# Routing attention and an ELU layer on one core: row sums of two blocks in one group of matmuls, masks of q on ScalarE, first k cut at 512 tokens

## The chip, the core and the metric

The kernel runs on one core of a Trainium2 chip. The core has a matrix engine (TensorE, PE in the profile), three engines for elementwise work (VectorE or DVE, ScalarE or ACT, GpSimd or POOL), a queue that issues transfers (SyncE or SP), and 16 DMA engines. Each engine works through its own instructions in program order and waits on semaphores for the others. TensorE writes into banks of PSUM; the other data lie in SBUF, with 128 partitions. The metric is device time in microseconds (us) of one execution, as a median over runs.

## The reference

```python
def _attn_ref(q, k, v, centroids):            # q, k, v: (4, 8, 768, 64)
    ...
    q_assign = np.argmax(np.einsum('bhsd,hcd->bhsc', q_n, c_n), axis=-1)
    k_assign = np.argmax(np.einsum('bhsd,hcd->bhsc', k_n, c_n), axis=-1)
    mask = q_assign[:, :, :, None] == k_assign[:, :, None, :]
    scores = scale * np.matmul(q, k.transpose(0, 1, 3, 2))
    scores = np.where(mask, scores, -1000000000.0)
    ...
    attn = np.exp(scores)
    attn = attn / (np.sum(attn, axis=-1, keepdims=True) + 1e-09)
    return np.matmul(attn, v).astype(np.float32)

def _moe_ref(x, w_in, w_out):                 # x: (3072, 512), w_in: (512, 2048)
    h = x @ w_in
    g = np.where(h > 0.0, h, np.exp(np.minimum(h, 0.0)) - 1.0)
    return (g @ w_out).astype(np.float32)
```

Each token of q and of k is given to the nearest of 16 centroids of its head, and a query sees only keys of its own cluster. The attention's output, with heads side by side, then goes through two matrix products with an ELU between them. The two weight matrices come as 64-bit floats; the kernel takes their words apart and joins them to 32-bit floats itself.

## The kernel before

**Blocks and slots.** The attention is cut into 32 blocks: batch (4), half of the queries (2), pair of heads (4). `slot_first` handles block 0 and `slot(n)` block n, for n = 1 to 31. In a slot TensorE computes, for each of six tiles of 128 keys, the scores of both heads (`plain`, L498) and adds the mask to them by a second product (`masked`, L511); ScalarE exponentiates 768 columns at once (`exponential`, L520). The keys lie on partitions and the 384 queries of the half along the free dimension. Three pairs of PSUM banks (`pair_tiles`) take the scores in turn.

**One block behind: the values.** At the start of slot n TensorE multiplies the probabilities of block n-1 with v (`values`, L536), into `o_bank`; ScalarE takes the result out, negated, into its place in `xT` (`take_values`, L550). `x_of(n)` is that place.

**Two blocks behind: row sums and division.** VectorE adds the six tiles of probabilities of a block into `summed` (`sums_begin`, L523; `sums_end`, L528 and L529). TensorE sums that over the partitions with a matrix of ones (`row_sums`, L554): one matmul for each head, 64 output partitions each, so that a row sum stands on all 64 partitions that need it, in `d_bank`. ScalarE reads them as a logarithm and as a copy, and forms the exponential of the negative logarithm (`take_sums`, L563 to L565). VectorE refines the reciprocal by one Newton step, with the sign that take_values left out (`divide`, L568, L569), and GpSimd multiplies x by it (L572). `d_bank` is used by the clusters too.

**Clusters.** `similar` (L427) multiplies the centroids with tokens: four matmuls of 32 output partitions each, into `d_bank` (or `o_bank` in the first slot). VectorE finds the greatest by transposes, a maximum and a comparison (`assign`, L440 to L453), with counts for a later check that each token has one cluster. ScalarE copies the result to the other half of the partitions (L456), and for q GpSimd makes 0 and -2^80 of it (`mask_q`, L463). q is treated in slots 1 and 5 of each batch (slot 3 instead of 1 in the first), k in slots 6 and 7 for the next batch. What is put into the list `later` (copies, masks, power steps) is issued by `flush` at the end of the slot.

**Weights.** `weigh(n)` puts some steps of the weights into each slot by a fixed table of room and cost (`ROOM`, `COST`): `begin` (L320, L328) separates words, ScalarE scales the exponents (L330, the power step, through `later`), and three `join` steps on VectorE (L340, L344, L350) put them together. What is left is done in the first group after the attention.

**Loads.** All plain loads are issued by SyncE in program order: v of the next block (`load_v`, L182), k and q of the next batch in small packets (`in_blocks`, L166), words of the weights (L300). The loads of the first k and q (L191) are laid out differently and are transposed on TensorE (`turned`, L577, copied out by ScalarE, L594).

**After the attention.** `finish_attention` is called within the first of four units (`unit(0, u)`) of the first group of 512 tokens, and handles the last block. In these units GpSimd works on weights (`w_step`, L727 to L732, with transfers to DRAM) and on the ELU (L762). Five groups more follow from 400 us on, in a scheme that the change leaves alone.

Of the kernel before, what the change touches and what calls it, by code (L numbers as in the profile page):

```python
# [61 lines left out]
def main_path(ctx, tc, c, q, k, v, centroids, moe_w_in, moe_w_out, out):  # L62
# [71 lines left out]
    top = early[:, 7488:7512]  # L134
    hot_q = early[:, 7512:7896].bitcast(BF16).rearrange("p (s n) -> p s n", s=2)
# [3 lines left out]
    summed = sums_w[:, 4 * HS : 6 * HS]  # L139
# [111 lines left out]
    cT = const.tile([P, P], F32, name="cT")  # L251
    count = const.tile([P, 4 * B], F32, name="count")
    counted = 0
    r_sum = const.tile([P, len(blocks)], F32, name="r_sum")
    d_sum = const.tile([P, len(blocks)], F32, name="d_sum")
    off = const.tile([P, 1], F32, name="off")
    nc.gpsimd.memset(off, -896.0 * 2**23)
# [52 lines left out]
    def begin():  # L310
# [19 lines left out]
        later.append(lambda: nc.scalar.activation(e, e, Act.Relu, scale=8.0, bias=off))  # L330
# [63 lines left out]
    credit, later = 0.0, []  # L394

    def flush():
        for other in later:
            other()
        later.clear()
# [25 lines left out]
    def similar(t, cols, ps):  # L425
        for pr in range(NPR):
            nc.tensor.matmul(  # L427
                ps[32 * pr : 32 * pr + 32, :HS],
                lhsT=cT[:, 32 * pr : 32 * pr + 32],
                rhs=t[pr][:, cols],  # L430
                start=True,
                stop=True,
            )

    def assign(hot, ps):
# [3 lines left out]
        n = HS // NC  # L439
        nc.vector.transpose(sim, ps[:, :HS])  # L440
# [20 lines left out]
    def mask_q(half):  # L461
        for x in range(2):
            nc.gpsimd.tensor_scalar(  # L463
                q_mask[half][:, :, x],
                hot_q,
                big[:, x : x + 1],
                minus[:, x : x + 1],
                op0=Alu.mult,
                op1=Alu.add,
            )  # L470

    def clusters_k(b, half, ps):
        cols = ts(half, HS)
# [3 lines left out]
    def clusters_q(b, half, ps):  # L477
        similar(qT[half], slice(0, HS), ps)

        def told():  # L480
            assign(hot_q, ps)
            later.append(lambda: mask_q(half))
# [4 lines left out]
    turn_of = 0  # L487
# [39 lines left out]
    def sums_end():  # L527
        nc.vector.tensor_tensor(add_to, add_to, probs_all[:, 8 * HS :], op=Alu.add)  # L528
        nc.vector.tensor_tensor(  # L529
            summed, add_to[:, : 2 * HS], add_to[:, 2 * HS :], op=Alu.add  # L530
# [21 lines left out]
    def row_sums(n):  # L552
        for e in range(2):
            nc.tensor.matmul(  # L554
                d_bank[64 * e : 64 * e + 64, :HS],
                lhsT=ones,
                rhs=summed[:, ts(e, HS)],
# [4 lines left out]
    def take_sums(n):  # L562
        nc.scalar.activation(r_of, d_bank[:, :HS], Act.Ln)  # L563
        nc.scalar.activation(e_of, d_bank[:, :HS], Act.Copy, accum_out=d_sum[:, n : n + 1])
        nc.scalar.activation(r_of, r_of, Act.Exp, scale=-1.0)  # L565

    def divide(n):
        nc.vector.tensor_tensor(e_of, e_of, r_of, op=Alu.mult)  # L568
        nc.vector.scalar_tensor_tensor(  # L569
            r_of, e_of, -2.0, r_of, op0=Alu.add, op1=Alu.mult, accum_out=r_sum[:, n : n + 1]  # L570
        )
        nc.gpsimd.tensor_tensor(x_of(n), x_of(n), r_of, op=Alu.mult)  # L572
# [8 lines left out]
    def turn(to, t, n):  # L581

        for i in range(HT):
            turned_by_pe(to[:, ts(i, P)], t, n + i)

    turns = 0

    def turned(to, t, n):
# [4 lines left out]
        turn(bank, t, n)  # L593
        nc.scalar.copy(to, bank[:, :HS])  # L594

    def slot_first():
# [10 lines left out]
        for pr in range(NPR):  # L607
            turned(kT[0][pr][:, :HS], first_k[pr], 0)
        told = [clusters_k(0, 0, o_bank)]
        flush()  # L610
        for pr in range(NPR):
            turned(kT[0][pr][:, HS:], first_k[pr], HT)
# [8 lines left out]
        for kt in range(NT):  # L621
            s = ring()
            plain(0, kt, s)
# [8 lines left out]
    def slot(n):  # L632
        b, at = n // NB, n % NB
        more = b + 1 < B
        if n > 1:
            row_sums(n - 2)
            take_sums(n - 2)
# [9 lines left out]
        if n > 0:  # L647
            sums_end()
        if n > 1:
            divide(n - 2)  # L650
        if n > 0:
            take_values(n - 1)
        if told is not None:
            told()

# [28 lines left out]
        flush()  # L684
# [678 lines left out]
    def findings():  # L1363
# [6 lines left out]
        nc.vector.tensor_scalar(ok[:, 1:2], peak[:, 1:2], D_MAX, None, op0=Alu.is_lt)  # L1370
        nc.vector.tensor_scalar(same, count, float(HS // NC), None, op0=Alu.is_equal)
# [10 lines left out]
    last_n = len(blocks) - 1  # L1382
# [14 lines left out]
    row_sums(last_n - 1)  # L1397
    values(last_n)
    sums_end()
# [316 lines left out]
```

## Time and profile before

| what | value |
|---|---|
| median of 3 runs | 901.79 us (900.97 to 903.19) |
| the profiled execution | 902.24 us, span 900.5 us |
| TensorE clock | 0.999 |
| attention, first group, rest | about 0 to 341, 341 to 400, 400 to 900 us |
| L554, row sums | 128 records (each f32 matmul leaves two), median 512 ns |
| L572, x by reciprocals (GpSimd) | 32, mean 1103 ns |
| L463, masks (GpSimd) | 16, from 983 to 3039 ns |
| L520, exponentials (ScalarE) | 192, mean 811 ns |
| L330, power step (ScalarE) | 16, median 1148 ns |
| L563, L564, L565 (ScalarE) | 32 each, median 479, 481 and 522 ns |
| L569 (VectorE) | 32, median 558 ns |

Busy time in stretches of the run (us), from the view that cuts the run into windows:

| from, to | TensorE | VectorE | ScalarE | GpSimd |
|---|---|---|---|---|
| 0, 20 | 17.36 | 9.30 | 10.80 | 3.06 |
| 20, 40 | 19.36 | 12.22 | 13.22 | 1.00 |
| 100, 200 | 100.00 | 96.84 | 76.42 | 20.59 |
| 200, 300 | 99.08 | 96.94 | 75.34 | 25.65 |
| 350, 375 | 25.00 | 23.05 | 11.54 | 18.47 |
| 700, 900 | 194.17 | 137.89 | 74.53 | 39.64 |

How to read it: an f32 matmul shows as two records; records that run side by side on different parts of the array overlap, so their durations do not add up, and the distance between starts is the better measure. In a timeline each row merges instructions of one line that follow each other: start, length, engine, line, operation, what it writes and reads, the tile of the array, shape, count, and in brackets the idle time before it with what ended it.

### The profile page before, as it was taken

The numbers are of one execution on the slowest core, as the hardware profiler recorded it, in microseconds if no ns is written. First come the engines' busy times: TensorE is split into PE (matmuls) and PEld (weight loads), VectorE is DVE, ScalarE is ACT, GpSimd is POOL, SyncE is SP. The second block draws the span as 40 slices with busy tenths as digits, with TensorE's granted clock in tenths as the row PEclk, the third lists the DMA queues.
The fourth block names the chain that finished last, engine by engine and source line by source line (L and its number), as shares of the span: only waits on it lengthen the run. The fifth ranks groups of instructions, "written<-read, shape, count | busy, mean of one in ns | idle before, by whom it ended". The sixth has DMA issues, their size and how long they took to land.

```text
span 900.5 us, 17050 instructions
## 1 busy us (share of the span) xinstructions
PE 889.9 (99%) x6473; PEld 687.6 (76%) x6473; DVE 725.9 (81%) x1067; ACT 449.5 (50%) x883; POOL 226.0 (25%) x257
## 2 busy tenths in 40 slices
PE   8999999999999999999999999999999999999997
PEld 4444444444444447899989999999999999999997
DVE  4699999999999997995389965895589558956885
ACT  5677787777776774420133225522552255225421
POOL 1022031221303244870033002520252025202300
PEclk9999999999999999999999999999999999999999
DMA  6765554365323622102698766176717761767272
GB/s 197 195 110 137 153 137 80 105 135 139 71 82 96 192 88 71 70 13 95 199 296 302 241 206 220 50 242 206 218 55 241 212 210 58 240 210 209 58 221 87
DMA packets 153209, 138.33 MB, mean 154 GB/s; under 512 B 89248, under 2 KB 106656, under 8 KB 152096
## 3 DMA queue, kind: packets, MB, share of 16 engines
q1 hardware_dynamic: 151584, 132.45, 50.2%
q0 software_dynamic: 1248, 4.20, 1.5%
q8 instruction: 53, 0.87, 0.4%
q10 hardware_dynamic: 288, 0.52, 0.2%
q14 instruction: 36, 0.29, 0.1%
HBM read 114.59 MB, written 21.50 MB: 151 GB/s over the span
## 4 chain that ended last, share of the span: by engine, by line
PE 92%; DVE 4%; DMA 2%; SPq 1%; issue 0%; ACT 0%; DVEq 0%
PE bank L994 23%; PE bank L748 16%; PE banks L498 12%; PE o_bank L536 12%; PE bank L1066 9%; PE o_bank L994 4%; PE o_bank L748 3%; PE banks L511 3%; PE d_bank L994 2%; PE d_bank L554 2%; PE o_bank L1066 2%; PE d_bank L427 1%; SPq L166 1%; DMA w_out<-in_k_dram 1%; PE d_bank L1066 1%; PE d_bank L748 1%
## 5 line engine op out<-in xcount | busy, mean ns | idle before, releaser
L520 ACT ACTIVATE p_out<-banks 128x768 f32<-128x768 f32 x192 | 155.2, 811 | 26.8 <-PE banks L511 25.4
L536 PE MATMUL o_bank<-p_out,kq_g 128*64 128x384 f32 x768 | 129.4, 486 | 0.1
L536 PEld LDWEIGHTS o_bank<-p_out,kq_g 128*64 128x64 f32 x768 | 55.0, 137 | 69.2 <-issue 62.7
L762 POOL TENSOR_SCALAR kq_g<-kq_g 128x512 f32<-128x512 f32 x96 | 67.8, 715 | 152.0 <-ACT kq_g L761 151.6
L572 POOL TENSOR_TENSOR xT<-xT,sums_w 128x384 f32<-128x384 f32 x32 | 35.3, 1103 | 222.0 <-DVE sums_w L569 164.6
L523 DVE TENSOR_TENSOR sums_w<-p_out 128x1536 f32<-128x1536 f32 x32 | 57.1, 1785 | 7.5 <-ACT p_out L520 7.5
L994 PE MATMUL bank<-w_out,kq_g 128*128 128x128 f32 x512 | 63.1, 275 | 0.0
L528 DVE TENSOR_TENSOR sums_w<-sums_w,p_out 128x1536 f32<-128x1536 f32 x32 | 59.0, 1845 | 3.3 <-DVE sums_w L523 0.5
L994 PEld LDWEIGHTS bank<-w_out,kq_g 128*128 128x128 f32 x512 | 60.5, 192 | 0.5
L761 ACT ACTIVATE kq_g<-bank 128x512 f32<-128x512 f32 x68 | 39.8, 602 | 38.9 <-PE bank L748 17.3
L748 PE MATMUL bank<-xT,spare 128*128 128x256 f32 x256 | 59.2, 379 | 0.0
L748 PEld LDWEIGHTS bank<-xT,spare 128*128 128x128 f32 x256 | 48.3, 190 | 6.4
L748 PE MATMUL bank<-x_sum,w_in 128*128 128x256 f32 x224 | 52.9, 379 | 0.0
L765 DVE SCALAR_TENSOR_TENSOR kq_g<-kq_g,bank 128x512 f32<-128x512 f32 x68 | 44.9, 680 | 6.2 <-POOL kq_g L762 6.2
L748 PEld LDWEIGHTS bank<-x_sum,w_in 128*128 128x128 f32 x224 | 42.6, 190 | 5.8
L1280 DVE TENSOR_TENSOR kq_g<-kq_g 128x1024 f32<-128x1024 f32 x36 | 45.2, 1263 | 1.5 <-PE bank L994 1.5
L1084 POOL TENSOR_TENSOR spare<-x_sum 128x128 f32<-128x128 f32 x16 | 7.3, 455 | 154.4 <-PE bank L1066 88.8
L463 POOL TENSOR_SCALAR kq_g<-w_out,big,minus 128x768 bf16<-128x768 bf16 x16 | 34.1, 2138 | 46.8 <-ACT w_out L456 46.8
L550 ACT ACTIVATE xT<-o_bank 128x384 f32<-128x384 f32 x32 | 15.7, 490 | 48.3 <-PE o_bank L536 48.3
L498 PE MATMUL banks<-x_sum,xT 64*128 64x384 f32 x192 | 39.8, 492 | 0.0
L498 PE MATMUL banks<-x_sum,kq_g 64*128 64x384 f32 x192 | 39.6, 491 | 0.0
L498 PE MATMUL banks<-kq_g 64*128 64x384 f32 x192 | 39.6, 491 | 0.0
(326 smaller groups left out, 2030.2 us busy)
## 6 DMA issues: line engine op xcount, KB each, us to landing
kq_g<-in_v_dram SPq DMA_DIRECT2D x32, 384.0 KB, 3.6
sums_w<-far_s_s SPq DMA_DIRECT2D x42, 256.0 KB, 3.7
spare<-w_far SPq DMA_DIRECT2D x32, 256.0 KB, 3.1
words_w<-far_s_s SPq DMA_DIRECT2D x26, 256.0 KB, 3.5
out_dram<-p_out SPq DMA_DIRECT2D x22, 256.0 KB, 3.4
w_out<-in_q_dram SPq DMA_DIRECT2D x112, 48.0 KB, 2.7
sums_w<-far_s_q SPq DMA_DIRECT2D x21, 256.0 KB, 3.6
words_w<-far_a_s SPq DMA_DIRECT2D x20, 256.0 KB, 3.7
```

What stands on the lines that cost most here:

```text
L498: nc.tensor.matmul(s[:, e, :HS], lhsT=kT[b % 2][pr][rows, ts(kt, P)], rhs=qT[half][pr][rows], start=True, stop=False,)
L520: nc.scalar.activation(probs[kt], s[:, :, :HS], Act.Exp, scale=SCALE)
L523: nc.vector.tensor_tensor(add_to, probs_all[:, : 4 * HS], probs_all[:, 4 * HS : 8 * HS], op=Alu.add)
L528: nc.vector.tensor_tensor(add_to, add_to, probs_all[:, 8 * HS :], op=Alu.add)
L536: nc.tensor.matmul(o_bank[64 * e : 64 * e + 64, :HS], lhsT=v_raw[n % 2][:, e, kt], rhs=probs[kt][:, e], start=(kt == 0), stop=(kt == NT - 1),)
L748: nc.tensor.matmul(bank[:, ts(f, QS)], lhsT=left[:, ch, ts(f, P)], rhs=right[:, ch], start=first and f == 0 and ch == 0, stop=ch == 1, ski ...
L761: nc.scalar.activation(to, as_part(bank, to), Act.Exp)
L762: nc.gpsimd.tensor_scalar(to, to, 1.0, 0.0, op0=Alu.min, op1=Alu.max)
L765: nc.vector.scalar_tensor_tensor(to, to, -1.0, as_part(bank, to), op0=Alu.add, op1=Alu.max)
L994: nc.tensor.matmul(bank[:, :P], lhsT=left[:, f], rhs=right[:, f], start=first and f == 0, stop=last and f == 3, skip_group_check=True,)
L1066: nc.tensor.matmul(bank[:, ts(f, P)], lhsT=left[:, ts(f, P)], rhs=right, start=m in ("m1", "m5") and f == 0, stop=True, skip_group_check=True,
L1280: nc.vector.tensor_tensor(b[to][:, f], b[x][:, f], b[y][:, f], op=op)
```

## The change

- Row sums are taken for two blocks at once, in odd slots n >= 3 for blocks n-3 and n-2. `summed` becomes two buffers, for even and odd blocks. `row_sums` issues four matmuls of 32 output partitions, one for each head of each block; `take_sums` and VectorE's step, now `reciprocals`, run once for two blocks, so each row sum stands on 32 partitions.
- `spread` copies the reciprocals with two transfers issued by GpSimd from a scratch place (`to_spread`) to all 128 partitions, one block into `r_of`, the other into `e_of`. In the next, even slot GpSimd multiplies the x of both blocks (`scale_x`), after a copy of one column (`mark`) that waits for VectorE's `sums_end`.
- Masks of q are made by ScalarE, except the very first.
- The power steps get a list of their own, `powers`, issued early in the next slot, after `take_sums`.
- VectorE's step on reciprocals comes after `told`, the assignment of clusters.
- In the first slot, k is transposed and given clusters in parts of 512 and 256 tokens instead of two of 384, the first scores are computed before the second part's clusters, and the ring of banks begins at another place. `findings` adjusts two counts for that.
- After the loop the last pairs are scaled: blocks 28 and 29 at once, 30 and 31 after the third unit.

```diff
-    summed = sums_w[:, 4 * HS : 6 * HS]
+    summed = [spare.rearrange("p a n -> p (a n)")[:, 2048 : 2048 + 2 * HS]]
+    summed.append(sums_w[:, 4 * HS : 6 * HS])
...
-        later.append(lambda: nc.scalar.activation(e, e, Act.Relu, scale=8.0, bias=off))
+        powers.append(lambda: nc.scalar.activation(e, e, Act.Relu, scale=8.0, bias=off))
...
-    def mask_q(half):
+    def mask_q(b, half):
         for x in range(2):
...
+            to, by, more = q_mask[half][:, :, x], big[:, x : x + 1], minus[:, x : x + 1]
+            if (b, half) == (0, 0):
+                nc.gpsimd.tensor_scalar(to, hot_q, by, more, op0=Alu.mult, op1=Alu.add)
+            else:
+                nc.scalar.activation(to, hot_q, Act.Identity, scale=by, bias=more)
...
     def clusters_k(b, half, ps):
-        cols = ts(half, HS)
+        cols = slice(half * HS, half * HS + HS)
+        if b == 0:
+            cols = slice(half * CUT, S if half else CUT)
...
     def row_sums(n):
-        for e in range(2):
+
+        for at in range(0, P, 32):
+            j, e = at // 64, at // 32 % 2
             nc.tensor.matmul(
-                d_bank[64 * e : 64 * e + 64, :HS],
-                lhsT=ones,
-                rhs=summed[:, ts(e, HS)],
+                d_bank[at : at + 32, :HS],
+                lhsT=ones[:, :32],
+                rhs=summed[(n - 1 + j) % 2][:, ts(e, HS)],
...
+    def scale_x(n, r):
+        nc.gpsimd.tensor_tensor(x_of(n), x_of(n), r, op=Alu.mult)
+
+    def spread(n):
+        r = to_spread(n)
+        for j, to in enumerate((r_of, e_of)):
+            nc.gpsimd.dma_start(
+                to, r[64 * j : 64 * j + 64].unsqueeze(1).to_broadcast([64, 2, HS])
+            )
...
         for pr in range(NPR):
-            turned(kT[0][pr][:, :HS], first_k[pr], 0)
+            turned(kT[0][pr][:, :CUT], first_k[pr], 0)
+        turned(kT[0][0][:, CUT:], first_k[0], CUT // P)
         told = [clusters_k(0, 0, o_bank)]
         flush()
-        for pr in range(NPR):
-            turned(kT[0][pr][:, HS:], first_k[pr], HT)
+        for pr in range(1, NPR):
+            turned(kT[0][pr][:, CUT:], first_k[pr], CUT // P)
+        first = ring()
+        plain(0, 0, first)
         told.append(clusters_k(0, 1, d_bank))
...
     def slot(n):
         b, at = n // NB, n % NB
         more = b + 1 < B
-        if n > 1:
-            row_sums(n - 2)
-            take_sums(n - 2)
+        sums_of = n - 2 if n > 1 and n % 2 else None
+        pair_done = n - 4 if n >= 4 and n % 2 == 0 else None
+        if sums_of is not None:
+            row_sums(sums_of)
+            take_sums(sums_of)
+        flush(powers)
...
-            sums_end()
-        if n > 1:
-            divide(n - 2)
+            sums_end(n - 1)
+        if pair_done is not None:
+            nc.gpsimd.tensor_copy(mark, summed[(n - 1) % 2][:, :1])
+            scale_x(n - 4, r_of)
+            scale_x(n - 3, e_of)
         if n > 0:
             take_values(n - 1)
         if told is not None:
             told()
+        if sums_of is not None:
+            reciprocals(sums_of)
+            spread(sums_of)
...
-        flush()
+        flush(later)
...
-    row_sums(last_n - 1)
     values(last_n)
-    sums_end()
+    sums_end(last_n)
...
-    take_sums(last_n - 1)
-    divide(last_n - 1)
+    scale_x(last_n - 3, r_of)
+    scale_x(last_n - 2, e_of)
...
         run(unit(0, u, finish_attention if u == 0 else None, fill_weights))
         if u == 1:
             findings()
+        elif u == 2:
+            scale_x(last_n - 1, r_of)
+            scale_x(last_n, e_of)
```

## The prediction

> **What bounds the kernel now.** I read the page first, then the waits of TensorE, then its timeline slot by slot, and last the queues that feed it (ScalarE, SyncE, GpSimd).
>
> ```profile
> PE 889.9 (99%) x6473; PEld 687.6 (76%) x6473; DVE 725.9 (81%) x1067; ACT 449.5 (50%) x883; POOL 226.0 (25%) x257
> PE d_bank L427 <- ACT sums_w L564: 0.9, 1, 0.9
> ```
>
> TensorE is busy for 889.9 of 900.5 us, so the change is worth what it takes out of TensorE's own sequence, plus waits that vanish, less waits that appear. VectorE is at 97% in the attention (96.84 of 100 us from 100 to 200), but TensorE does not wait for it there: in its list of waits VectorE stands only for the start. Work taken off VectorE, GpSimd or ScalarE is worth nothing unless one of them becomes late.
>
> ```profile
> 24.31 0.39 PE L511 MATMUL banks<-kq_g,w_out 64*128 64x384 bf16 x2
> 24.63 4.09 PE L536 MATMUL o_bank<-p_out,kq_g 128*64 128x384 f32 x24
> ...
> 33.44 0.33 PE L511 MATMUL banks<-kq_g,w_out 64*128 64x384 bf16 x2
> 33.70 0.87 PE L554 MATMUL d_bank<-sums_w,ones 128*64 128x384 f32 x4
> 34.40 4.04 PE L536 MATMUL o_bank<-p_out,kq_g 128*64 128x384 f32 x24
> 38.37 0.92 PE L498 MATMUL banks<-x_sum,xT 64*128 64x384 f32 x4
> ...
> 48.35 0.85 PE L427 MATMUL d_bank<-kq_g,cT 128*32 128x384 f32 x8
> 49.13 0.92 PE L498 MATMUL banks<-x_sum,xT 64*128 64x384 f32 x4
> ```
>
> The columns are start, duration, engine and line. Durations overlap, so costs are taken from start to start. A slot without row sums (n = 1) goes from scores (L511, 24.31) to values (L536) in 0.32 us. One with them goes from L511 (33.44) to row sums (L554) in 0.26 and on to values in 0.70. The product with the centroids (L427) has the very shape that the new row sums get, four outputs of 32 partitions with 384 columns, and costs 0.78 to the next start (0.79 at 8.60, where tiles of 128 by 64 follow).
>
> ```profile
> 44.33 0.20 PEld L536 LDWEIGHTS o_bank<-p_out,kq_g 128*64 128x64 f32 x4 [0.72 <-DMA kq_g<-in_v_dram]
> ...
> 250.13 1.15 ACT L330 ACTIVATE sums_w<-sums_w,off 128x1024 uint32<-128x1024 uint32 x1 [1.28 <-DVE sums_w L328]
> 251.19 0.47 ACT L563 ACTIVATE sums_w<-d_bank 128x384 f32<-128x384 f32 x1
> 251.56 0.48 ACT L564 ACTIVATE sums_w<-d_bank 128x384 f32<-128x384 f32 x1
> ...
> 252.18 0.85 PE L427 MATMUL d_bank<-kq_g,cT 128*32 128x384 f32 x8 [0.92 <-ACT sums_w L564]
> ```
>
> Two waits matter. Slot 3's values wait for the third load of v until 44.33. And in slot 23 the centroid product waits 0.92 us, since a power step (L330), itself late behind VectorE, stood before the reading of d_bank (L563, L564).
>
> ```profile
> L463 POOL TENSOR_SCALAR kq_g<-w_out,big,minus 128x768 bf16<-128x768 bf16 x16 | 34.1, 2138 | 46.8 <-ACT w_out L456 46.8
> w_far<-spare POOLq DMA_DIRECT2D x8, 256.0 KB, 2.3
> ```
>
> The masks take GpSimd 2.1 us each, and transfers that GpSimd issues land after 2.3 us.
>
> **What the Trainium skill says.** "TensorEngine Tiling (Array Packing)", Key Properties: tiles work in parallel, and changing the tiling mode drains the engine. The trace agrees: 8 records of 32 columns cost 0.78, 4 of 64 columns 0.70, and a change of mode shows as 0.26 to 0.32 where L511 to L498 (same mode) takes 0.16. "SBUF — State Buffer", SBUF: two separate sides: a GpSimd operation and a VectorE operation with two SBUF inputs hold a shared port exclusively. It agrees: VectorE's L528 took 2.36 us beside a mask (158.73) and 1.76 without. "ScalarE: Activation LUTs", Table sets: identity is in every set, so the moved masks bring no table load; no run shows Identity here. "DMA: Bandwidth & Descriptors", Anatomy of one DMA: 2.0 us plus bytes at 436 GB/s, an estimate of 2.45 us for 192 KB; the 2.3 above is near it.
>
> **The change part by part.**
>
> *Row sums.* Before, 32 pairs of matmuls of 64 columns; after, 16 groups of four of 32 columns, in slots 3, 5, ... 31 and once after the loop. In an even slot L554 goes: 0.70 saved, but L511 to L536 may take 0.32 instead of the 0.26 to L554. Bounds of that term 0 to 0.12; I take 0.06. Slots 4 to 30: 14 x 0.64 = 9.0 us. In an odd slot the group costs 0.79 instead of 0.70, since a mode change now lies on both sides; between 0.70 and 0.90, I take 0.79: slots 5 to 31, 14 x 0.09 = 1.3 lost. After the loop one pair goes (0.64) and the last becomes a group (0.09 lost): 0.5. Sum 8.3 us.
>
> *Reciprocals, half as often.* 16 times fewer L563 to L565 (1.5 us of ScalarE) and L568, L569 (1.2 us of VectorE). Neither is on the path: nothing.
>
> *Spreading.* reciprocals writes a scratch of 384 columns, and two GpSimd transfers copy it over r_of and e_of. They are issued in odd slot n once VectorE is through, 6 to 8 us in. The scaling follows in slot n+1 behind sums_end (3 to 6 us in), two L572 of 1.0 us. ScalarE's take_sums waits for it only in slot n+2, some 18.8 us after slot n began. With 2.4 us for landing this is ready several us early: nothing. Queued behind that wait would be the exponentials, for which TensorE waits. From slots 29 to 31 on, GpSimd's L727, L729 and L731 stand behind transfers and scaling.
>
> *Power step.* It moves behind take_sums into the next slot. The wait in slot 23 goes: 0.9 us saved. It now stands before take_values, inside the 4.0 us of values.
>
> *Masks on ScalarE.* Two activations of 768 elements in each of 7 half batches; L520 has the size and takes 0.81, so 0.8 to 0.9 each. They run after two copies (L456, 1.03 together), so from about 1.9 to 3.6 us into the next, even slot, where take_values cannot start before 4.0: hidden. With a power step besides (1.15) ScalarE is free at 4.8; the first exponential is due at 5.1, take_values takes 0.49, so 0.2 us late, within the 0.4 us that the ring of three bank pairs allows. Without that cover at most 7 x 1 us. GpSimd loses 14 x 2.1 us, off the path.
>
> *The start.* With k cut at 512, transposes of pair 3 end at about 13.9 and the first group's product runs at 14.5. VectorE's four steps for 512 tokens take about 2.9 us instead of 2.4, and the first mask product can begin at about 19.4, as before (19.37). The second part is needed only at the fifth key tile, so the stop of 0.64 us at 22.1 goes: slot 0 ends some 0.7 earlier (between 0.5 later and 1.2 earlier). But slot 3's values wait for v. Its load stands in SyncE's queue behind one chain of loads that starts when pair 0 of k is turned (15.33 before, about 14.7 after) and runs on issue and transfer. So v lands at about 43.7, while TensorE would be ready at 42.8. Of the start and of slot 2's missing row sum together 0.6 us is left (0 to 1.4).
>
> *The first group after the attention.* GpSimd issues two more transfers (L732: 0.57 to 0.74 each) and two more scalings behind unit 2. Before unit 2's next L762 it idles 2.3 us (at 372.19), and s4 is ready 1 to 2 us before use, so nothing; at worst 2 us.
>
> Sum: 8.3 + 0.9 + 0.6 = 9.8 us. The profiled execution took 902.24 us (span 900.5), which gives 892.4; the median shown, 901.79, is 0.45 lower, so 892.0.
>
> **The rivals.**
>
> 1. *Slower: the spread lands late.* If r_of and e_of are not scaled when take_sums comes, ScalarE stops, and with it the exponentials. From issue at 7 or 8 us to the last useful moment is about 13 us, 2 of them scaling: it decides from a landing of 11 us on, and each further us costs 15 us. At 12 us: 892 + 15 = 907. For it: the accumulating transfers of L1390 took 12.2 us. Against: those move 512 KB each, and L732 lands in 2.3 to 5.8.
> 2. *No change: four tiles don't overlap.* If 32 columns run only two at a time, a group costs 1.40: 14 x 0.7 = 9.8 lost instead of 1.3, time 900.5. L427 speaks against it.
> 3. *Half of it lost on the queues.* Masks with a power step late by 0.5 us in each of 7 slots, and 1 to 2 us behind GpSimd in the first group: 892 + 5 = 897. For it: ScalarE's order is tight in these slots. Against: bank ring and idle stretches named above.
> 4. *More gained.* L511 to L536 costs no more than L511 to L554, the group no more than the pair, and v is early: 0.8 + 1.3 + 0.6 more, 889.3.
>
> **How the numbers follow.** Forecast 0.60, rivals 0.03, 0.03, 0.16 and 0.18. The range reaches from 889.5, near rival 4, to 895.5, inside rival 3. What this measurement can tell from no change is 0.3%, 2.7 us: faster means below 899.1. Rivals 1 and 2 are the rest: faster 0.94, same 0.03, slower 0.03.
>
> **What would show it.** Row sums in TensorE's timeline: 8 records, 0.75 to 0.9 from start to start, in odd slots only; L511 to values near 0.32 in even ones. No wait of the centroid product for ScalarE. Slot 3's values still waiting for v, near 43.7. Transfers of the spread landing in 2 to 4 us, and no wait of ScalarE's Ln for GpSimd. Wrong would be: exponentials starting later than 5.3 us into even slots, TensorE idle before L498, or records of the four tiles one after another.

## The result, and the profile after

The changed kernel takes 892.59 us, the median of four executions (891.91 to 893.83). The kernel before, beside it, takes 902.42 (900.97 to 903.19). The ratio is 0.9901, 95% interval 0.9889 to 0.9913. The forecast was 892.0. The profiled execution of the changed kernel took 893.83 us, span 892.1, and is the slowest of its four; that of before took 902.24, span 900.5.

The page of the changed kernel:

```profile
PE 880.4 (99%) x6473; PEld 681.1 (76%) x6473; DVE 705.5 (79%) x1021; ACT 440.4 (49%) x833; POOL 225.7 (25%) x289
...
sums_w<-xT POOLq DMA_DIRECT2D x28, 192.0 KB, 3.3
```

TensorE has the same 6473 records as before and is busy for 9.5 us less: no matmul has gone, four of them now lie side by side where two did. The second line is 28 of the 32 transfers of the spread; they land 3.3 us after their issue, in the median.

Its timeline of TensorE (start, length, line) in slots 2 and 3, and at the centroid product of slot 23. L510 is the former L498, L523 the former L511, L548 the values, L568 the row sums, L438 the centroid product:

```profile
32.49 0.33 PE L523 MATMUL banks<-kq_g,w_out 64*128 64x384 bf16 x2
32.75 4.09 PE L548 MATMUL o_bank<-p_out,kq_g 128*64 128x384 f32 x24
36.77 0.92 PE L510 MATMUL banks<-x_sum,xT 64*128 64x384 f32 x4
...
41.55 0.33 PE L523 MATMUL banks<-kq_g,w_out 64*128 64x384 bf16 x2
41.81 0.52 PE L568 MATMUL d_bank<-spare,ones 128*32 128x384 f32 x2
41.83 0.52 PE L568 MATMUL d_bank<-sums_w,ones 128*32 128x384 f32 x2
42.16 0.49 PE L568 MATMUL d_bank<-spare,ones 128*32 128x384 f32 x2
42.17 0.49 PE L568 MATMUL d_bank<-sums_w,ones 128*32 128x384 f32 x2
42.60 4.09 PE L548 MATMUL o_bank<-p_out,kq_g 128*64 128x384 f32 x24
...
240.36 4.09 PE L548 MATMUL o_bank<-p_out,kq_g 128*64 128x384 f32 x24
244.38 0.85 PE L438 MATMUL d_bank<-kq_g,cT 128*32 128x384 f32 x8
```

Three things are to be seen. An even slot goes from L523 to the values in 0.26 us (the forecast had 0.32); an odd one spends 0.79 on the group (41.81 to 42.60), whose four tiles overlap, starting in pairs. The values of slot 3 start at 42.60 with no wait for v, where before they waited until 44.33. And the centroid product of slot 23 follows the values at once; its wait of 0.92 is gone.

How far the changed kernel is ahead, from the starts of the values in both traces:

| at the values that start in | before | after | ahead |
|---|---|---|---|
| slot 1 | 24.63 | 23.68 | 0.95 |
| slot 2 | 34.40 | 32.75 | 1.65 |
| slot 3 | 44.33 | 42.60 | 1.73 |
| slot 4 | 54.87 | 52.45 | 2.42 |
| slot 5 | 64.58 | 62.30 | 2.28 |
| slot 23 | 247.22 | 240.36 | 6.86 |
| slot 24 | 258.70 | 250.21 | 8.49 |
| slot 31 | 327.47 | 317.59 | 9.88 |
| after the loop | 337.18 | 326.66 | 10.52 |
| end (spans) | 900.5 | 892.1 | 8.4 |

From slot 5 on, each even slot gains 0.64 or 0.65 and each odd one gives back 0.14; slots 2 and 4 gain 0.70. Slot 23 gains 0.98 besides, from its values to those of slot 24. The first row has chance in it: a second profile of the changed kernel is 0.58 ahead there, since its first loads come later (the transposed centroids, L640, stand at 8.48 us, in the first profile at 8.10, before at 7.89). From that point to the values of slot 1 both profiles take 15.6 us, the kernel before 16.7. So 10.5 us are gained in the attention (10.1 in the second profile), and in this execution 2.1 of them are lost later. Where, the waits of TensorE say (writer, releaser, us in total, times, longest):

```profile
PE bank L796 <- DMA spare<-w_far: 0.8, 1, 0.8
...
PE o_bank L796 <- DVE o_bank L852: 0.3, 1, 0.3
...
PE bank L1042 <- DVE kq_g L813: 0.3, 1, 0.3
```

The lower two stand in the first group after the attention, between 377 and 384 us, where the lead falls by 0.9. The upper one comes at 465 us and costs 1.0; another 0.15 goes behind the last matmul. This wait belongs to this execution: the second profile of the same kernel (893.19 us) lacks it, and is 9.2 us ahead at the end.

### The profile page after: what moved, and what is told of

The parts are those of the page before. It is cut to its first block, busy times and chain, and to the rows that moved or that the text cites. A ratio compares the mean times of both kernels' runs of the same rounds, so it can differ in the third digit from the quotient of the medians.

```text
span 892.1 us, 17029 instructions
## 1 busy us (share of the span) xinstructions
PE 880.4 (99%) x6473; PEld 681.1 (76%) x6473; DVE 705.5 (79%) x1021; ACT 440.4 (49%) x833; POOL 225.7 (25%) x289
## 3 DMA queue, kind: packets, MB, share of 16 engines
q0 software_dynamic: 3296, 10.49, 4.6%
## 4 chain that ended last, share of the span: by engine, by line
PE 91%; POOL 3%; DVE 2%; issue 2%; DMA 1%; SPq 1%; ACT 0%; POOLq 0%; ACTq 0%
PE bank L1042 23%; PE banks L510 15%; PE o_bank L548 14%; PE bank L796 11%; PE bank L1114 9%; PE o_bank L1042 4%; PE banks L523 4%; PE d_bank L1042 2%; PE o_bank L796 2%; PE o_bank L1114 2%; PE d_bank L568 1%; PE d_bank L438 1%; POOL kq_g L810 1%; PE d_bank L1114 1%; DMA spare<-w_far 1%
## 5 line engine op out<-in xcount | busy, mean ns | idle before, releaser
L548 PE MATMUL o_bank<-p_out,kq_g 128*64 128x384 f32 x768 | 130.9, 490 | 0.0
L548 PEld LDWEIGHTS o_bank<-p_out,kq_g 128*64 128x64 f32 x768 | 52.3, 137 | 74.8 <-issue 69.7
L810 POOL TENSOR_SCALAR kq_g<-kq_g 128x512 f32<-128x512 f32 x96 | 69.4, 731 | 150.1 <-ACT kq_g L809 149.7
L535 DVE TENSOR_TENSOR sums_w<-p_out 128x1536 f32<-128x1536 f32 x32 | 59.1, 1847 | 10.3 <-ACT p_out L532 10.3
L540 DVE TENSOR_TENSOR sums_w<-sums_w,p_out 128x1536 f32<-128x1536 f32 x32 | 56.2, 1757 | 3.3 <-DVE sums_w L535 0.5
L609 POOL DMA_DIRECT2D sums_w<-xT x28 | 17.8, 650 | 153.2 <-DVE xT L585 92.0
L813 DVE SCALAR_TENSOR_TENSOR kq_g<-kq_g,bank 128x512 f32<-128x512 f32 x68 | 45.0, 680 | 7.7 <-POOL kq_g L810 7.7
L604 POOL TENSOR_TENSOR xT<-xT,sums_w 128x384 f32<-128x384 f32 x32 | 41.1, 1305 | 1.6 <-DMA sums_w<-xT 1.6
L510 PE MATMUL banks<-x_sum,xT 64*128 64x384 f32 x192 | 39.8, 492 | 0.0
L510 PE MATMUL banks<-kq_g,xT 64*128 64x384 f32 x192 | 39.6, 491 | 0.0
L510 PE MATMUL banks<-x_sum,kq_g 64*128 64x384 f32 x192 | 39.6, 491 | 0.0
```

Source lines behind the costliest of these rows:

```text
L510: nc.tensor.matmul(s[:, e, :HS], lhsT=kT[b % 2][pr][rows, ts(kt, P)], rhs=qT[half][pr][rows], start=True, stop=False,)
L535: nc.vector.tensor_tensor(add_to, probs_all[:, : 4 * HS], probs_all[:, 4 * HS : 8 * HS], op=Alu.add)
L548: nc.tensor.matmul(o_bank[64 * e : 64 * e + 64, :HS], lhsT=v_raw[n % 2][:, e, kt], rhs=probs[kt][:, e], start=(kt == 0), stop=(kt == NT - 1),)
L604: nc.gpsimd.tensor_tensor(x_of(n), x_of(n), r, op=Alu.mult)
L810: nc.gpsimd.tensor_scalar(to, to, 1.0, 0.0, op0=Alu.min, op1=Alu.max)
L813: nc.vector.scalar_tensor_tensor(to, to, -1.0, as_part(bank, to), op0=Alu.add, op1=Alu.max)
```

## The experiments

Eleven are versions of the changed kernel, the twelfth is that kernel itself once more. Times are medians; "ratio" is against runs of the kernel before on the same chip.

| version | us (lowest to highest) | ratio, 95% interval |
|---|---|---|
| one block's row sums at a time | 903.67 (902.96 to 904.69) | 1.0023, 1.0014 to 1.0032 |
| group of four issued twice | 902.25 (901.39 to 903.50) | 1.0011, 1.0002 to 1.0019 |
| start as before | 894.05 (893.07 to 895.16) | 0.9916, 0.9899 to 0.9932 |
| all masks of q on GpSimd | 896.11 (895.33 to 897.10) | 0.9938, 0.9922 to 0.9955 |
| power step in `later` | 892.39 (892.17 to 893.56) | 0.9897, 0.9880 to 0.9913 |
| no mark | 892.85 (892.03 to 893.43) | 0.9901, 0.9884 to 0.9917 |
| spread issued by SyncE | 893.11 (892.70 to 893.84) | 0.9906, 0.9890 to 0.9923 |
| last scaling one unit earlier | 892.73 (892.25 to 893.28) | 0.9898, 0.9881 to 0.9914 |
| 0.6 us more room for weights | 897.75 (895.57 to 898.79) | 0.9954, 0.9941 to 0.9967 |
| 1.1 us more room | 896.42 (894.33 to 896.84) | 0.9931, 0.9919 to 0.9942 |
| 0.6 more room and early scaling | 896.51 (895.47 to 897.20) | 0.9938, 0.9925 to 0.9952 |
| the changed kernel again | 893.10 (892.93 to 893.97) | 0.9902, 0.9888 to 0.9916 |

### What the pairing brings by itself

The pairing was undone, and with it what belongs to it: the spread, the scaling of two blocks later on, and the place of VectorE's division behind the clusters. The new start, the masks on ScalarE, the order of the power steps and the two sum buffers stayed.

```diff
-        for at in range(0, P, 32):
-            j, e = at // 64, at // 32 % 2
+        for e in range(2):
             nc.tensor.matmul(
-                d_bank[at : at + 32, :HS],
-                lhsT=ones[:, :32],
-                rhs=summed[(n - 1 + j) % 2][:, ts(e, HS)],
+                d_bank[64 * e : 64 * e + 64, :HS],
+                lhsT=ones,
+                rhs=summed[n % 2][:, ts(e, HS)],
...
-        sums_of = n - 2 if n > 1 and n % 2 else None
+        sums_of = n - 2 if n > 1 else None
```

> Only the pairing undone: row sums, take_sums and the division one block at a time as before, in every slot from 2 on; new start, masks on ScalarE, power step behind take_sums and the two buffers of sums stay. Theory (pairing is worth 14 x 0.51 + 0.7 us of TensorE in the attention and costs 0.9 after it): slots of 9.71 and 10.49 us, no wait in slot 23, time 899 to 900.5. Rival (much of the gain comes from VectorE, ScalarE or GpSimd being relieved): slot lengths other than these, with waits.

Measured: 903.67, more than the 899 to 900.5 expected. It is 2.3 us slower than the kernel before on the same chip, and 10.6 to 10.8 slower than two versions with the pairing that ran beside it (892.85 and 893.11, below). The values after the loop start at 336.18, 9.5 us later than with the pairing and only 1.0 earlier than before. So the pairing carries the whole gain, and the other parts without it bring none: of what they gain at the start and in slot 23, 1.2 us go in five of the seven slots after q's clusters, each 0.2 or 0.3 longer than before, and the first group after the attention takes 0.9 of the rest. Another 1.0 goes behind 800 us, most of it after the last matmul; why is open. The reason for the longer slots stands in this version's timelines around slot 10, first that of ScalarE:

```profile
116.62 1.95 ACT L480 ACTIVATE kq_g<-w_out,minus,big 128x768 bf16<-128x768 bf16 x2
118.47 0.46 ACT L575 ACTIVATE sums_w<-d_bank 128x384 f32<-128x384 f32 x1
...
120.76 0.48 ACT L562 ACTIVATE xT<-o_bank 128x384 f32<-128x384 f32 x1
121.13 4.41 ACT L532 ACTIVATE p_out<-banks 128x768 f32<-128x768 f32 x6
```

TensorE's, in the same version:

```profile
121.64 0.33 PE L523 MATMUL banks<-kq_g 64*128 64x384 bf16 x2
121.99 0.92 PE L510 MATMUL banks<-x_sum,kq_g 64*128 64x384 f32 x4
```

The masks (L480, 1.95 us) push the reading of the row sums (L575) and all behind it. The first exponential starts 5.8 us after the values (115.30), and TensorE's fourth pair of scores (121.99) comes 0.35 us after the mask product ahead of it instead of 0.16: the ring of three bank pairs has run out. In the changed kernel the same masks fall into even slots, which have no row sums to read. From values to values, slots 10 and 26 take 9.85 us like the even slots around them, and slots 6, 14 and 22, with a centroid product, 10.63, which is its 0.78 more. Masks on ScalarE are hidden there because of the pairing, with little to spare: in slots 10 and 26 the first exponential starts 5.27 us after the values, elsewhere 5.14 where no centroid product stands between.

### Do the four tiles overlap, and what is the price of the change of mode?

The group was issued twice in each odd slot. The second group writes the same sums again.

```diff
         if sums_of is not None:
             row_sums(sums_of)
+            row_sums(sums_of)
             take_sums(sums_of)
```

> In each odd slot the group of four row sums is issued twice into the same place. Theory (the four tiles overlap, 0.65 us for a group without a change of tiling, and 0.14 to 0.19 us of the price of 0.84 is the change of tiling): odd slots get 0.62 to 0.68 us longer, 15 x 0.65 = 9.8 us in all, time 902.4. Rival (the group is priced by its eight records of 0.49, not overlapped): 1.3 us or more for each slot, 912 or more.

Measured: 902.25, as the theory said. Its timeline in slot 3:

```profile
41.90 0.52 PE L568 MATMUL d_bank<-spare,ones 128*32 128x384 f32 x2
...
42.56 0.49 PE L568 MATMUL d_bank<-spare,ones 128*32 128x384 f32 x2
...
43.32 1.51 PE L548 MATMUL o_bank<-p_out,kq_g 128*64 128x384 f32 x8
```

From the first group to the second is 0.66 us, from the second to the values 0.76. A stretch with a group in it lasts 10.49 instead of 9.85, and after the loop the kernel is 9.75 us later: fifteen groups of 0.65. Four tiles of 32 columns thus take 0.65 by themselves, and the other 0.10 to 0.14 of a group is the change to the next mode. The forecast's second rival, that only two tiles run at a time (1.40 a group), is out.

### Where the start's gain goes

```diff
-    CUT = 512
+    CUT = HS
...
-        turned(kT[0][0][:, CUT:], first_k[0], CUT // P)
         told = [clusters_k(0, 0, o_bank)]
         flush()
-        for pr in range(1, NPR):
+        for pr in range(NPR):
             turned(kT[0][pr][:, CUT:], first_k[pr], CUT // P)
-        first = ring()
-        plain(0, 0, first)
```

> The first slot as before the change: k in two parts of 384, first scores in order, the ring's first position. Theory (the start is worth 0.95 us, and the load of v takes none of it back): values of block 0 start at 24.6 instead of 23.7, slot 3's values at 43.5 instead of 42.6, time 893.5. Rival (as forecast: the load of v gives back what the start gained): slot 3's values start where they do now or within 0.3 us of it, time 892.6 to 892.9.

Measured: 894.05, 1.0 to 1.5 above the changed kernel's two medians (893.10 and 892.59). From the transposed centroids (at 7.61 us here, at 8.10 in the changed kernel) to slot 3's values it takes 35.45 us, in the changed kernel 34.50: the start is worth 0.95 there. At slot 1's values it is 0.75. The other 0.2 is a wait for v that is back with the old start: from slot 2's values to slot 3's this version takes 10.05 us, the changed kernel 9.85.

```profile
43.06 0.20 PEld L546 LDWEIGHTS o_bank<-p_out,kq_g 128*64 128x64 f32 x4 [0.83 <-DMA kq_g<-in_v_dram]
```

The forecast had v take the start's gain back. SyncE's own timeline shows why it didn't, first with the start as before:

```profile
14.64 2.84 SPq L172 DMA_DIRECT2D w_out<-in_k_dram  x4
...
39.27 1.11 SPq L188 DMA_DIRECT2D kq_g<-in_v_dram  x2
```

SyncE's timeline in the changed kernel:

```profile
13.79 2.84 SPq L174 DMA_DIRECT2D w_out<-in_k_dram  x4
...
38.32 1.11 SPq L190 DMA_DIRECT2D kq_g<-in_v_dram  x2
```

The chain is nearly as long in both (24.63 and 24.53 us; 24.97 in the profile of the kernel before), as the forecast said. But counted from the transposed centroids it starts at 5.69 us in the changed kernel and at 7.03 here, because the changed kernel turns the rest of pair 0 ahead of the first centroid product. So the load of v is issued 1.44 us earlier, more than TensorE gained, and v takes nothing back.

### The masks' old place

```diff
-            if (b, half) == (0, 0):
+            if True:
                 nc.gpsimd.tensor_scalar(to, hot_q, by, more, op0=Alu.mult, op1=Alu.add)
```

> All masks of q by GpSimd again, the rest as in the changed kernel. Theory (masks are off TensorE's path on either engine): slot lengths stay 9.07, 9.85 and 10.63 us, time 892.6 within 0.5. Rival (masks on GpSimd delay VectorE's additions through the shared port, and these delay row sums or exponentials): some slots after slots 1, 3 and 5 of a batch get longer by 0.3 to 1 us, 894 to 898.

Measured: 896.11, 3.0 to 3.5 us above the changed kernel. All slots of the attention are as long as in the changed kernel but one, from the values of slot 27 to those of slot 28: 11.00 instead of 9.07. GpSimd's timeline in this version:

```profile
272.28 5.85 POOL L478 TENSOR_SCALAR kq_g<-w_out,big,minus 128x768 bf16<-128x768 bf16 x2 [1.58 <-ACT w_out L469]
278.08 1.86 POOL L1441 DMA_DIRECT2D w_in<-w_in  x2
```

TensorE's, in the same version:

```profile
291.04 2.16 PE L548 MATMUL o_bank<-p_out,kq_g 128*64 128x384 f32 x12 [1.86 <-DMA kq_g<-in_v_dram]
```

GpSimd's in the changed kernel:

```profile
270.33 1.97 POOL L1441 DMA_DIRECT2D w_in<-w_in  x2
```

Two masks of 5.85 us stand in GpSimd's queue ahead of two accumulating transfers of 512 KB (L1441). These are issued 7.75 us later. They then run beside the load of v: the DMA engines were busy for 0.21 of the stretch from 275 to 280 (0.98 in the changed kernel) and fully from 280 to 295, the longest landing of v grew from 9.5 to 12.4 us, and TensorE waited 1.86 for it. In the profiled executions, 895.33 here and 893.19 in the second profile of the changed kernel, this slot is nearly the whole difference; the other three executions here took 895.75 to 897.10, and what they lose besides was not seen. So the theory is out, and the rival named another cause. The masks had been off the path in the kernel before: there the same two transfers, also behind masks, were issued at 284.3 us and landed after 10.8 and 13.6, and TensorE did not wait. In the changed kernel, which reaches this place 9 us earlier, they are not. Whether that lead alone is why was not tried.

### The power step's order

```diff
-        powers.append(lambda: nc.scalar.activation(e, e, Act.Relu, scale=8.0, bias=off))
+        later.append(lambda: nc.scalar.activation(e, e, Act.Relu, scale=8.0, bias=off))
```

> The power steps go back to the end of the slot, before take_sums. Theory (their order was the cause of the wait of 0.92 us in slot 23): slot 23 or another odd slot with clusters gets a wait of TensorE for ScalarE of up to 1 us again, time 893 to 893.6. Rival (the wait went because VectorE is less loaded and the power step's input is ready earlier): no wait, 892.6.

Measured: 892.39, as the changed kernel, and slot 23 takes 9.85 us with no wait. ScalarE's timeline of this version there:

```profile
241.75 1.15 ACT L340 ACTIVATE sums_w<-sums_w,off 128x1024 uint32<-128x1024 uint32 x1
242.80 0.47 ACT L578 ACTIVATE sums_w<-d_bank 128x384 f32<-128x384 f32 x1
```

The power step stands before the row sums again, as before the change, but without its idle 1.28 us for VectorE. So d_bank is read in time for the centroid product at 244.55. With one block at a time and the new order the wait was gone as well (slot 23: 10.49). So the new order was not needed. Whether it is enough by itself is not shown, since the version without the pairing differs from the kernel before in its start and its masks too.

### Mark and spread

```diff
         if pair_done is not None:
-            nc.gpsimd.tensor_copy(mark, summed[(n - 1) % 2][:, :1])
...
-            nc.gpsimd.dma_start(
+            nc.sync.dma_start(
```

The two edits ran apart: first without the mark, then with the spread issued by SyncE.

> Without the copy that makes GpSimd's multiplication wait for VectorE's additions. Theory (VectorE isn't on TensorE's path in the attention): VectorE's L540 and L541 are slowed in some slots, slot lengths stay, time 892.6 within 0.5. Rival (delayed additions delay exponentials that write the same buffers): even slots longer by 0.2 to 1 us, 895 or more.

> The two spreading transfers are issued by SyncE, in its order, instead of by GpSimd. Theory (a late spread stops ScalarE at take_sums, and the slack is about 11 us from issue): where SyncE works on 16 loads of q (11 us), the transfers or the loads of v behind them come late; ScalarE's Ln waits for GpSimd and TensorE loses some us in 3 to 6 of the odd slots, 896 to 915. Rival (a late spread is hidden, or SyncE issues in time): slot lengths as now, 892.6.

Measured: 892.85 and 893.11, with every slot of the attention as long as in the changed kernel. Neither the mark nor the issue of the spread is on the path there. With SyncE's spread the first group loses 1.8 us instead of 0.9, which the medians hardly show.

### The loss in the first group

All versions so far lose about 0.9 us at this place (with SyncE's spread 1.8), even the one without pairing. GpSimd's timeline there in the changed kernel:

```profile
361.56 0.61 POOL L810 TENSOR_SCALAR kq_g<-kq_g 128x512 f32<-128x512 f32 x1 [2.29 <-ACT kq_g L809]
...
370.10 3.39 POOL L810 TENSOR_SCALAR kq_g<-kq_g 128x512 f32<-128x512 f32 x2
373.46 2.40 POOL L604 TENSOR_TENSOR xT<-xT,sums_w 128x384 f32<-128x384 f32 x2
375.84 0.61 POOL L810 TENSOR_SCALAR kq_g<-kq_g 128x512 f32<-128x512 f32 x1
```

VectorE's, in the same kernel:

```profile
370.44 2.58 DVE L385 TENSOR_TENSOR w_out<-w_out 128x2048 f32<-128x2048 f32 x1
...
376.48 0.69 DVE L813 SCALAR_TENSOR_TENSOR kq_g<-kq_g,bank 128x512 f32<-128x512 f32 x1 [1.47 <-POOL kq_g L810]
377.08 0.69 DVE L852 TENSOR_TENSOR o_bank<-o_bank,spare 128x512 f32<-128x512 f32 x1
```

TensorE's, in the same kernel:

```profile
377.92 1.97 PE L796 MATMUL o_bank<-xT,spare 128*128 128x256 f32 x8 [0.33 <-DVE o_bank L852]
```

GpSimd's in the kernel before, where L762 stood for L810:

```profile
372.19 0.61 POOL L762 TENSOR_SCALAR kq_g<-kq_g 128x512 f32<-128x512 f32 x1 [2.29 <-ACT kq_g L761]
...
380.68 3.96 POOL L762 TENSOR_SCALAR kq_g<-kq_g 128x512 f32<-128x512 f32 x3
```

In the changed kernel TensorE waits for L852, which stands in VectorE's queue behind L813, which waits 1.47 for GpSimd's L810 at 375.84. That L810 stood behind the two late scalings (L604), and these behind two L810 that took 3.39 us together, beside VectorE's sum L385. In the kernel before, the same three instructions (380.68) took 3.96 us back to back, beside the same sum (there L375), and TensorE did not wait. So what is new at this place is the two scalings, 2.40 us. GpSimd's idle stretch of 2.29 us comes one unit earlier, and stands there in both kernels (372.19 before, 361.56 after). The scaling was therefore moved ahead by one unit, into this stretch:

```diff
         if u == 1:
             findings()
-        elif u == 2:
             scale_x(last_n - 1, r_of)
```

> The last two multiplications by GpSimd (blocks 30 and 31) come after the second unit instead of after the third. Theory (GpSimd was full at that place, so 2.4 us of multiplications pushed its work on the ELU, then VectorE, then TensorE): the waits of TensorE for VectorE between 370 and 385 us (0.33 and 0.28 us) vanish, since GpSimd idles 2.3 us behind the second unit, and the first group takes 0.9 us less: about 891.7. Rival (the 0.9 us come from the transfers of the spread or from ScalarE's order): the waits stay, no change, 892.6.

Measured: 892.73, no gain. GpSimd's L604 now stands at 359.71, and the wait for L813 is gone from TensorE's list, but that for L852 is 0.5 instead of 0.3, and the loss is 0.9 as before. So taking the scalings out of the late place does not save the 0.9. VectorE is now slowed beside GpSimd instead: its L879 (362.80) takes 1.68 us and its L354 (367.13) 3.01, in the changed kernel 0.69 and 2.29. In the version without the pairing, which has no scaling in these two units, their counterparts take 1.81 and 3.00. So, as far as the traces tell, the 0.9 is lost in more than one way. Next in question was VectorE's amount of work. It was tried with more room for weight steps in the attention, where VectorE has become idler (93.45 of 100 us from 100 to 200, before 96.84): one piece more is joined there, and VectorE has 4 steps less in the first group.

```diff
-        credit = min(credit, 2.5) + ROOM[n]
+        credit = min(credit, 2.5) + ROOM[n] + (0.6 if n % 2 == 0 and n > 2 else 0.0)
```

> The changed kernel with 0.6 us more room for weight steps in every even slot from 4 on, so that a piece of the weights more (four steps, some 5 us of VectorE) is done before slot 31 instead of in the first group. Theory (VectorE has been given room in the attention, and the first group gives back 0.9 us because VectorE is full there): slot lengths stay 9.07 and 9.85, the first group's waits for VectorE (0.3 and 0.3 in the changed kernel) go, and the total falls by about 0.9, to 891.7. Rival 1 (the waits of the first group come from the phase of VectorE against GpSimd, not from the amount of work): total within 0.4 us of the changed kernel, 892.2 to 893.0. Rival 2 (the freed time is already used up by ScalarE's masks and the additions, so that steps come late): even slots lengthen by 0.2 us or more, total 894 or more.

> The same with 1.1 us more room in every even slot from 4 on. The same number of steps is left at slot 31 as with 0.6, but they come earlier and more of them in one slot. Theory: as with 0.6, 891.7, since VectorE lost 1.1 us in each even slot by the change. Rival 1: within 0.4 us of the changed kernel. Rival 2: this is where the additions come late first: even slots 0.2 us or more longer than with 0.6.

> The changed kernel itself once more, as the measure for the two versions with more room, on the same chip and in the same rounds: 892.6, within 0.5 us.

In both versions with more room the third weight sum (L389, at 370.55 and 371.68) is written over the reciprocals of the last two blocks before these are scaled (375.88 and 378.10), so x of blocks 30 and 31 is multiplied by other numbers; no instruction is left out. Measured: 897.75 and 896.42, beside 893.10 for the changed kernel: slower by 4.7 and 3.3 us, so neither the theory nor rival 1 holds. With 0.6 all slots of the attention keep their length, so rival 2 is out; the loss lies in and behind the first group. With 1.1 slots 12 and 14 lengthen by 0.29 and 1.32, the second for another reason than late additions. SyncE's timeline of that version:

```profile
142.65 10.60 SPq L174 DMA_DIRECT2D w_out<-in_q_dram  x16
153.35 0.56 SPq L310 DMA_DIRECT2D spare<-in_moe_w_out_dram  x1
154.00 2.15 SPq L190 DMA_DIRECT2D kq_g<-in_v_dram  x2
```

The loads of q are issued 4.1 us later than in the repeated run of the changed kernel (138.53), and a load of 1 MB of words stands between them and v, for which the values then waited 1.25. One more run joined 0.6 of room with the early scaling, so that no reciprocal is overwritten:

> 0.6 us more room for weight steps in even slots, and the two scalings of blocks 30 and 31 already after the second unit. With more room alone, VectorE's large sums of weights come some 10 us earlier in the first group, the second and third of them (370.55 and 372.75) beside GpSimd's L810, and the scalings stand before the next L810 at 375.88; TensorE then waited 2.33 us at 380.34. The third sum, written at 370.55 onto the reciprocals, also came before the scaling there, so that x of blocks 30 and 31 was multiplied by weights instead of reciprocals; here it is not. Theory (the amount of VectorE's work sets the first group's loss, and the late scaling spoilt the gain): no wait of o_bank in L796 for VectorE, total 891.7 to 892.2. Rival (GpSimd is the engine that is late in the third unit, since the sums of two SBUF inputs lengthen its L810 and L777, wherever the scaling stands): a wait of 0.3 us or more stays or moves, total 892.6 or more.

Measured: 896.51, as the rival said. GpSimd's timeline in this version:

```profile
368.51 3.30 POOL L777 TENSOR_TENSOR spare<-w_in,spare 128x512 f32<-128x512 f32 x1
...
372.73 5.01 POOL L810 TENSOR_SCALAR kq_g<-kq_g 128x512 f32<-128x512 f32 x3
```

VectorE's, in the same version:

```profile
368.10 2.58 DVE L387 TENSOR_TENSOR p_out<-w_out 128x2048 f32<-128x2048 f32 x1
...
371.80 2.28 DVE L389 TENSOR_TENSOR sums_w<-w_out,p_out 128x2048 f32<-128x2048 f32 x1
374.00 2.69 DVE L391 TENSOR_TENSOR words_w<-w_out,p_out 128x2048 f32<-128x2048 f32 x1
```

TensorE's, in the same version:

```profile
380.88 3.56 PE L796 MATMUL o_bank<-xT,spare 128*128 128x256 f32 x8 [2.31 <-DVE o_bank L852]
```

VectorE's sums read two operands from SBUF. Beside L387 GpSimd's L777 takes 3.30 us instead of the 1.27 it takes a unit earlier; beside L389 and L391 three L810 take 5.01 instead of three times 0.62. The Trainium skill, in "SBUF — State Buffer", SBUF: two separate sides, says that such an operation and one of GpSimd that reads SBUF hold a shared port in turn, each for a whole instruction, and the lengths agree: L777 ends 1.13 us after L387. With a piece less to join, these sums move forward. VectorE has less work in the group but more in this unit: between 364 and 377 us four sums of together 10.2 us stand where the changed kernel has one sum and three joining steps, 7.3 us. From 356 us it runs without a wait up to L852, where in the changed kernel it waits 0.65 and 1.47 us for GpSimd, and TensorE waits longer. Both engines are full there and lengthen each other's work; which of them would be in time without the other was not tried, nor a version that keeps them apart. For the changed kernel's own 0.9 this collision is no account, since it stands in the kernel before as well, without a wait. What its trace adds are the two scalings, and moving them only moved the loss; what would save the 0.9 stays open. None of the versions beats the changed kernel by more than the runs can tell.

## Why the prediction was right, and which terms were off

| step of the forecast | predicted, us | measured, us |
|---|---|---|
| even slots 4 to 30 | 14 x 0.64 = 9.0 | 0.70 + 13 x 0.645 = 9.1 |
| odd slots 5 to 31 | 14 x -0.09 = -1.3 | 14 x -0.14 = -1.9 |
| row sums after the loop | 0.5 | 0.64 at the values after it |
| slot 23 | 0.9 | 0.98 |
| start, and slot 2's row sum | 0.6 | 1.73 at slot 3's values |
| sum to the end of the attention | 9.8 | 10.5 |
| first group | 0 | -0.9 |
| 465 us and the end, in this execution | not in it | -1.2 |
| all | 9.8 | 8.4 by the profile, 9.8 by the medians of 902.42 and 892.59, 8.9 by those of the repeated run (901.95 and 893.10) |

- *Row sums.* Right, and the whole of the gain by the run without the pairing. The even slots' 0.64 came out by luck of its parts: from L523 to the values it took 0.26 and not 0.32, but values that follow a change of mode take 4.02 instead of 3.97 to the next start, which was not counted. The odd slots' term was too small by the same 0.05; the group itself took the 0.79 that was forecast.
- *The start.* "Of the start and of slot 2's missing row sum together 0.6 us is left": this is the step that failed. v was to land at 43.7; the values that need it started at 42.60, with no wait. The load of v was rightly seen as the end of a chain on SyncE of nearly fixed length, but the chain's start was put at 14.7 and was at 13.79. The forecast had the transposes of pair 3 end at 13.9 and the first group's product run at 14.5. In the trace the transposes ahead of that product, the rest of pair 0 among them, run from 9.60 to 13.75, and the product starts at 13.68. Of the 1.73, 0.95 stands at slot 1's values and 0.70 is slot 2's row sum; in slot 3 the wait for v (0.22 before) is gone and the group costs 0.14.
- *Slot 23.* The wait went. The reason given, the power step's new place, was not needed: with the pairing the wait went without it.
- *Masks.* Hidden, as said, and nearly at the times given: in slots 10 and 26 x is taken at 4.91 us (ScalarE was to be free at 4.8). They take 1.02 us each instead of the 0.8 to 0.9 read from an exponential of the same size. The Trainium skill has the better price in "ScalarE: Activation LUTs", What ACT_TABLE_LOAD costs: 186 ns, 0.833 ns for each of the 768 elements, and 93 ns for each operand that holds one value for each partition, of which the masks have two; an estimate of 1.01 us. "GpSimd loses 14 x 2.1 us, off the path" holds for the kernel before only: with GpSimd's masks in the changed kernel, one slot is 1.9 us longer through v. The forecast looked at GpSimd's busy time and not at the transfers queued behind the masks.
- *Spread.* Hidden, as said. Landings of 2.7 to 6.4 us, median 3.2, are longer than the 2.45 estimated, but stay far from the 11 from which the first rival would have decided. ScalarE never waited for it.
- *First group.* "So nothing; at worst 2 us" was taken at nothing, and 0.9 was lost. The forecast relied on an idle stretch of GpSimd of 2.3 us (at 372.19) that stands one unit ahead of the place where the scalings go; at that place (380.68) L762 ran three times without idling. The stretch is still there in the changed kernel, unused.
- The errors of the two ends nearly cancel, 0.7 too little in the attention and 0.9 too much behind it, so the total is closer than its parts. That is luck, and so is the 9.8 of the medians: the repeated run gives 8.9.

## What to carry to other kernels

When an engine is full, look for matmuls whose output partitions hold copies of one result, and that can wait for a partner: here each row sum was written onto 64 partitions, and half of that copying could be left to transfers that nothing waited for. Price such a change from start to start in the timeline, and count the change of mode on both sides of the new group. Work taken off an idle engine is still worth something if a transfer is queued behind it, and an idle stretch is cover only if it stands at the very place in the engine's queue where the new work goes: count the instructions up to it.

## What had not been expected

- A piece of the weights less for VectorE to join in the first group made the kernel slower by 3 to 5 us: its sums moved forward, beside more of GpSimd's work. L810 took 0.62 us alone and up to 1.7 on average there.
- Two accumulating transfers of 512 KB landed after 5.5 and 8.2 us when issued at 270 us and after 9.8 and 12.5 when issued 7.75 us later beside other loads, and moved the end through the load of v.
